# Second batch's kept-pair transpositions ordered after the first batch's last probabilities on VectorE

## The chip, the cores and the metric

The kernel runs on one core of one Trainium2 chip. The metric is the device time of one execution in microseconds (us). Three runs of the kernel before gave 949.78, 950.34 and 950.64 us; the median is 950.34 us. TensorE (PE in the profile) multiplies matrices into accumulators in PSUM; VectorE (DVE), ScalarE (ACT) and GpSimd (POOL) work on elements; SyncE (SP) issues transfers (DMA) between memory and the core's SBUF. Every engine executes its own instructions in the order in which the program lists them, and waits where an operand is not there yet.

## The reference

Eight batches of attention (8 heads, 576 positions, width 64) are followed by a gated feed-forward layer over all 4608 tokens. Heads 0 to 3 see the last 32 positions, heads 4 to 7 see every 32nd position back from their own.

```python
scores = scale * np.matmul(q, k.transpose(0, 1, 3, 2))
mask_local = (rel >= 0) & (rel < stride)                      # heads 0..3, stride = 32
mask_strided = (rel >= 0) & (pos[None, :] % stride == pos[:, None] % stride)   # heads 4..7
attn = softmax(np.where(masks, scores, -1e9))
x = np.matmul(attn, v) -> [4608, 512]
h = x @ w_in                                                  # 512 -> 2048
g = h * np.clip(h + 3.0, 0.0, 6.0) / 6.0
out = g @ w_out                                               # 2048 -> 512
```

## The kernel before

**Work units.** Two heads make a pair, four pairs (c = 0 to 3) a batch; pair g is numbered through the batches, so g = 0 to 3 is the first batch and g = 4 to 7 the second. Within the second batch `TURNS` takes the strided pairs first: g = 4 is c = 2 and g = 5 is c = 3. Pairs 0 to 7 go through `kept_pair`, the rest through `pair`. For the feed-forward layer a batch is a tile of 512 tokens (the 64 left over of every batch are collected in `left`), which `ffn` takes in 16 chunks fc of 128 hidden units. Exactness near fp32 is had by splitting every operand into a high and a low part, so that a product is three matmuls: L973, L974, L975 (tile `ph`, the first product) and L931, L932, L933 (tile `acc`, the second).

**A pair's steps in `kept_pair`.** Query and key are loaded (L360, tiles `qn` and `kn`, into one of three buffers `n`) and, for the second batch, transposed on VectorE (`tr`, L492: `qt<-qn` and `kplain<-kn` or `kt<-kn`). For the first batch TensorE transposes them instead. TensorE makes the scores (L551, L554, tile `ps`; two banks of PSUM for the second batch), ScalarE copies the wanted blocks (L568), GpSimd masks them (L587), VectorE takes the maximum (L592), GpSimd subtracts it (L596), ScalarE exponentiates (L599), VectorE sums and inverts (L602 to L607), GpSimd normalises (L611). VectorE then transposes the probabilities in four pieces (`transposes`, L637, tile `atkept<-e`), one set for each head j of the pair, and TensorE multiplies them with the values (L689, tile `pv`). In `keep_x` the result is split: ScalarE writes the high part of `x` (L396), VectorE the low part (L399), first for one half of the tokens and then for the other, in a chain.

**The first tile of `ffn`.** The four first products fc = 0 to 3 are begun before all four pairs are there: each collects the pairs c in the order 0, 2, 1, 3 as they come. fc = 0 and 1 use the two `ph` banks, fc = 2 and 3 the banks of the accumulators 2 and 3:

```python
pk = ("acc", fc) if t == seq[0] and fc in (2, 3) else ("ph", fc % 2)
```

Each then goes through `gated` (ScalarE L985 `u<-ph`, VectorE L989 `u<-u,ph`, called the gate below) and `parts_of` (ScalarE L997 `gh`, GpSimd L1002 `gl`). Only when the gate of fc = 2 has read its bank can the second product write accumulator 2; the second product of one fc is four groups of three matmuls, for accumulators 0 to 3.

**Weights.** A chunk of weights comes as fp32 (L287, `rawi` and `rawo`), is cut apart by ScalarE (L295, L299), joined by VectorE (L303, called a join below), rounded on ScalarE or GpSimd (L309, L311), and GpSimd makes the low part (L315).

**The order is written by a planner.** `Plan.op` records each operation with its engine, its cost, the names of what it reads and writes, a due time, an earliest planned time (`early`) and a further distance to what it depends on (`room`). `Plan.emit` runs a list schedule over these costs: of the engines it takes the one that can start soonest, and there the operation that can start soonest, at equal starts the one with the earlier due time. From one operation to the next there are 0.12 us (0.02 us on the same engine) in this planner's clock, to which `room` is added. The operations are then emitted in the order of their planned starts, and that is the order of each engine's instructions on the chip; the planned times themselves do not reach the chip. The names are free: a name that stands for no tile orders operations in the plan and makes no semaphore.

For the transpositions of query and key `room` is `LATE` = 2.0 and `early` is the later of `due - AHEAD` and `T0 + OPEN`, for g = 4 the planned 50.0. Transfers are planned with 2.2 us (`FETCH`) and a further time of their own between issue and landing.

Of the kernel before, what the change touches and what calls it, by code (L numbers as in the profile page):

```python
# [32 lines left out]
AHEAD = 27.0  # L33
PTPE = 0
BYACT = 8
OPEN = 6.0
# [4 lines left out]
T0 = 44.0  # L41
TILE = 98.5
ROOM = 1.2
LATE = 2.0
# [7 lines left out]
class Plan:  # L52
# [12 lines left out]
    def op(self, engine, us, fn, reads=(), writes=(), due=0.0, room=0.0, mode="", after=0.0, take=None, give=None, early=0.0):  # L65
        n = len(self.ops)
        before = set()
        for k in reads:
            if k in self.wrote:
                before.add(self.wrote[k])  # L70
            self.used.setdefault(k, []).append(n)
        for k in writes:
            if k in self.wrote:
                before.add(self.wrote[k])
            before.update(self.used.pop(k, ()))
            self.wrote[k] = n
        before.discard(n)
        how = engine if isinstance(engine, dict) else {engine: us}
        self.ops.append((how, fn, before, due, room, mode, after, take, give, early))
        return n  # L80
# [85 lines left out]
def attention_ffn(ctx: ExitStack, tc, q, k, v, w_in, w_out, out):  # L166
# [6 lines left out]
    NPAIR = H // 2  # L173
# [14 lines left out]
    op = plan.op  # L188
# [82 lines left out]
    def wkey(w, g, i):  # L271
        return ("w", w, g, i)
# [58 lines left out]
    def psum(key, name):  # L331
        return new(pp, key.key if isinstance(key, Slot) else key, [P, TOK], F32, name)
# [13 lines left out]
    def timing(g):  # L346
        b = g // NPAIR
        if not b:
            return T0 - 6.0 * (NPAIR - g)
        return wanted[b] - 6.0 - (NPAIR - 1 - g % NPAIR) * (wanted[b] - opens[b]) / NPAIR  # L350
# [57 lines left out]
    def kept_pair(g):  # L408
# [3 lines left out]
        loc = h0 < H // 2  # L412
        nm = f"{b}_{c}"
        early = (b == 0) + (g == 0)
        due = timing(g)
# [8 lines left out]
        tkey = {"q": qkey, "k": kkey}  # L424
# [17 lines left out]
        for x in "qk":  # L442
            if early:
                nkey = wkey("io"[x == "k"], NQ - 2, c)
            else:
                nkey = ("n", nn[0] % 3)
                nn[0] += 1

            if early:

                def load(x=x, nkey=nkey):
                    t = new(wp, nkey, [P, NQB, 2, D], F32, f"{x}n{nm}")
                    for j in range(2):
                        (nc.scalar if g == 1 else nc.sync).dma_start(
                            t[:QB, :, j], {"q": q, "k": k}[x][b, h0 + j].rearrange("(i p) d -> p i d", p=QB))
                tb = [slot(early) for _ in range(2)]

                def tr(x=x, nkey=nkey, tb=tb):
                    ps = [psum(tb[h], f"{x}p{nm}{h}") for h in range(2)]
                    for i in range(NQB):  # L460
                        nc.tensor.transpose(ps[i // 3][:, i % 3 * QB:i % 3 * QB + QB],
                                            tiles[nkey][:QB, i].rearrange("p j d -> p (j d)"), tiles["ident",][:QB, :QB])

                def evac(e, x=x, tb=tb, h=0):
                    ps, to, half = tiles[tb[h].key][:, :S // 2], qk_of(x), NPOS // 2
                    if loc:
                        c0 = (PAD if x == "k" else 0) + S // 2 * h
                        to = to[:, c0:c0 + S // 2]
                    else:
                        to = to.rearrange("c (r m) -> c m r", r=STRIDE)[:, half * h:half * h + half]  # L470
                        ps = ps.rearrange("c (m r) -> c m r", r=STRIDE)
                    if e == "ACT":
                        nc.scalar.copy(to, ps)
                    else:
                        nc.vector.tensor_copy(to, ps)
                op("ACT" if g == 1 else "SP", 1.06, load, writes=[nkey], due=-60 + 2 * g + (x == "k") - 900 * (g == 1), after=0.9)
                op("PE", 0.13 * NQB * slow, tr, reads=[("ident",), nkey, "plain", tkey[x]], writes=tb, take=tb, due=due - 1020, mode="s")
                for h in range(2):
                    op({"ACT": 0.45, "DVE": 0.4} if loc else {"ACT": 0.65, "DVE": 0.65}, 0, partial(evac, h=h), reads=[tb[h]],
                       writes=[tkey[x]] if h == 0 else [tkey[x] + (1,) if isinstance(tkey[x], tuple) else tkey[x] + "1"], give=tb[h], due=due - 19)  # L480
                continue

            def load(x=x, nkey=nkey):
                load_qk(x, b, h0, nkey, ap, f"{x}n{nm}")

            def tr(x=x, nkey=nkey):
                to = qk_of(x)
                if loc:
                    to = to[:, PAD if x == "k" else 0:].rearrange("c (m r) -> c m r", r=STRIDE)
                else:  # L490
                    to = to.rearrange("c (r m) -> c m r", r=STRIDE)[:, :NPOS]
                nc.vector.transpose(to, tiles[nkey])  # L492
            op("SP", 2.12, load, writes=[nkey], due=due - 35, early=due - 45, after=2.0)
            op("DVE", 0.8 if loc else 1.25, tr, reads=[nkey, "plain"], writes=[tkey[x]], due=due - 18, early=max(due - AHEAD, T0 + OPEN), room=LATE)


        vkey = wkey("i", NQ - 1, c) if early else ("vt",) if loc else wkey("i", NQ - 1, odd)
# [17 lines left out]
        ekeys = [("el" if loc else "es", j) for j in range(2)]  # L515
        akeys = [("atl", j) for j in range(2)] if loc else [wkey("o", NQ - 1, 0)] * 2
# [18 lines left out]
        for j in range(2):  # L535
# [6 lines left out]
            for i0 in range(0, nblk, 4):  # L542
# [14 lines left out]
                def keep(e, j=j, bkey=bkey, blocks=blocks, i0=i0):  # L557
# [16 lines left out]
                first = i0 == 0  # L574
# [6 lines left out]
                   writes=[ek, st] if first else [ek + (i0,)], give=bkey, due=sd + 0.5)  # L581
# [44 lines left out]
        def transposes(j):  # L626
            def tr():
                at, e = tiles[akeys[j]], e_whole(j)
                if loc:
                    for a in range(3):  # L630
                        for h in range(2):
                            nc.vector.transpose(at[PAD * (a + h):PAD * (a + h) + PAD, :, PAD * a:PAD * a + PAD],
                                                e[PAD * a:PAD * a + PAD, :, PAD * h:PAD * h + PAD])
                else:
                    for a in range(4):
                        rows = slice(PAD * a, PAD * a + PAD)
                        nc.vector.transpose(at[rows, :, rows], e[rows])  # L637

            def whole(half, key):
                ps = psum(key, f"pp{nm}{j}{half}").rearrange("p (u x) -> p u x", x=P)  # L640
                for u in range(nblk // 2):
                    i = half * nblk // 2 + u
                    if loc:
                        nc.tensor.transpose(ps[:2 * PAD, u, :QB], e_whole(j)[:, i], tiles["ident",][:QB, :QB])
                    else:
                        nc.tensor.transpose(ps[:PAD, u], e_whole(j)[:, i], tiles["ident",])

            def parts(half, key):
                ps = tiles[key.key].rearrange("p (u x) -> p u x", x=P)[:, :nblk // 2]
                at = tiles[akeys[j]][:, half * nblk // 2:(half + 1) * nblk // 2]  # L650
                if loc:
                    for a in range(3):
                        for h in range(2):
                            nc.scalar.copy(at[PAD * (a + h):PAD * (a + h) + PAD, :, PAD * a:PAD * a + PAD],
                                           ps[PAD * h:PAD * h + PAD, :, PAD * a:PAD * a + PAD])
                else:
                    for a in range(4):
                        nc.scalar.copy(at[PAD * a:PAD * a + NPOS, :, PAD * a:PAD * a + NPOS],
                                       ps[:NPOS, :, PAD * a:PAD * a + NPOS])
            if j == 0 and g < PTPE:  # L660
                for half in range(2):
                    tb = slot(early)
                    op("PE", 0.08 * slow * nblk / 2, partial(whole, half, tb), reads=[("ident",), ekeys[j]], writes=[tb, akeys[j]], take=tb,
                       due=due - 1002, room=0.0 if early else ROOM, mode="s")
                    op("ACT", 6 * 0.3 if loc else 4 * 0.25, partial(parts, half, tb), reads=[tb], writes=[akeys[j]], give=tb, due=due - 2 + j)
            else:
                op("DVE", 6 * 0.37 if loc else 4 * 0.435, tr, reads=[ekeys[j]], writes=[akeys[j]], due=due - 2 + j)

        if loc:
            transposes(0)  # L670
# [2 lines left out]
            def both():  # L673
                window_products(psum(vb[0], f"pv{nm}0"), psum(vb[1], f"pv{nm}1"), tiles[vkey], [tiles[x] for x in akeys])
            op("PE", 1.3 * slow, both, reads=[*akeys, vkey], writes=[*vb, *xk, lk], take=vb, due=due - 1001,
               room=0.0 if early else ROOM, mode="v")
            keep_x(nm, b, c, [(vb[0], lambda ps: ps, lambda x: x, TOK, False),
                              (vb[1], lambda ps: ps[:, :LEFT], lambda x: x, LEFT, True)], due)
        else:
            for j in range(2):  # L680
                transposes(j)

                def mm(j=j):
# [8 lines left out]
                   due=due - 1001 + j, room=0.0 if early else ROOM, mode="v")  # L692
# [420 lines left out]
```

## Time and profile before

| what | value |
|---|---|
| device time, three runs | 949.78, 950.34, 950.64 us |
| the profiled execution: span from first to last instruction | 949.4 us |
| TensorE busy | 930.3 us (98%) |
| VectorE, ScalarE, GpSimd busy | 593.4, 521.6, 446.0 us |
| the first 80 us: TensorE busy, granted clock | 66.78 us, 0.85 |

Of the profiled execution the span is recorded; its time is that span and what lies around it, which the runs put at 0.4 to 1.2 us (949.78 or 950.64 less 949.4). In the timelines that follow, a row is a start, a duration, an engine, the line of the kernel, the operation, the tile written and the tiles read, and how many instructions are merged; square brackets hold the idle time of that engine just before and what ended it. A row of windows gives a stretch, its length, the busy time of the engine with the number of instructions, the granted TensorE clock as a share of full speed, the share of the DMA engines in use, and GB/s.

### The profile page before, as it was taken

How to read it: one execution, taken by the hardware profiler on the slowest of the kernel's cores; microseconds unless marked ns; L12 is line 12 of the kernel's file. 1: busy time of each engine (PE TensorE's matmuls, PEld its weight loads, DVE VectorE, ACT ScalarE, POOL GpSimd, SP SyncE). 2: the span in 40 equal slices, each digit the busy share in tenths (PEclk: the TensorE clock that was granted, in tenths of full speed). 3: DMA queues.
4: the chain of work that ended last, by engine and by line, in shares of the span. 5: the costliest groups of instructions: out<-in, count | busy, mean ns of one | idle time of the engine just before them, and what ended most of it. 6: DMA issues, size and time to landing. Idle time of an engine off the chain costs nothing.

```text
span 949.4 us, 15283 instructions
## 1 busy us (share of the span) xinstructions
PE 930.3 (98%) x5084; PEld 772.1 (81%) x5084; DVE 593.4 (63%) x1644; ACT 521.6 (55%) x1325; POOL 446.0 (47%) x441
## 2 busy tenths in 40 slices
PE   8869999999999999999999999999999999999997
PEld 8657787888888788988888888888888888888896
DVE  6966677778868776556577687677786873111111
ACT  5747857766665556455346665666556553322332
POOL 5646888554535344434345454544453552222221
PEclk9968999999999999999999999999999999999999
DMA  9658630322222123112112322232223200100000
GB/s 209 211 152 234 159 86 1 86 39 42 52 74 49 32 39 80 22 34 56 27 19 48 72 42 40 42 84 42 40 42 84 42 14 1 45 1 1 33 13 22
DMA packets 197190, 57.16 MB, mean 60 GB/s; under 512 B 188408, under 2 KB 188408, under 8 KB 197112
## 3 DMA queue, kind: packets, MB, share of 16 engines
q1 hardware_dynamic: 194744, 55.61, 25.9%
q10 hardware_dynamic: 2368, 0.59, 0.4%
q8 instruction: 40, 0.66, 0.3%
q14 instruction: 38, 0.31, 0.1%
HBM read 46.73 MB, written 9.44 MB: 59 GB/s over the span
## 4 chain that ended last, share of the span: by engine, by line
PE 91%; SPq 3%; DMA 3%; issue 1%; ACT 1%; DVE 0%; POOL 0%; POOLq 0%; ACTq 0%; DVEq 0%
PE acc L931 13%; PE ph L973 12%; PE acc L932 12%; PE acc L933 12%; PE ph L974 12%; PE ph L975 12%; PE ps L808 3%; PE pv L379 2%; DMA rawi<-in_moe_w_in_dram 2%; PE phl L973 2%; PE phl L975 2%; PE phl L974 2%; PE accl L933 1%; PE accl L931 1%; PE accl L932 1%; PE pv L883 1%
## 5 line engine op out<-in xcount | busy, mean ns | idle before, releaser
L1002 POOL TENSOR_TENSOR gl<-u,gh 128x512 fp32r<-128x512 f32 x128 | 168.8, 1319 | 298.6 <-ACT gh L997 265.1
L973 PE MATMUL ph<-x,wi 128*128 128x512 f32 x512 | 204.3, 399 | 0.0
L931 PE MATMUL acc<-wo,gh 128*128 128x512 f32 x512 | 201.6, 394 | 0.0
L974 PE MATMUL ph<-x,wi 128*128 128x512 f32 x512 | 201.2, 393 | 0.2 <-DVE x L399 0.2
L975 PE MATMUL ph<-x,wi 128*128 128x512 f32 x512 | 201.0, 393 | 0.0
L932 PE MATMUL acc<-wo,gh 128*128 128x512 f32 x512 | 200.0, 391 | 0.0
L933 PE MATMUL acc<-wo,gl 128*128 128x512 f32 x512 | 200.0, 391 | 0.0
L985 ACT ACTIVATE u<-ph,three 128x512 f32<-128x512 f32 x128 | 88.3, 690 | 168.4 <-PE ph L975 167.4
L989 DVE SCALAR_TENSOR_TENSOR u<-u,ph 128x512 f32<-128x512 f32 x128 | 87.7, 686 | 131.4 <-ACT u L985 130.2
L832 ACT ACTIVATE e<-e,st 126x126 f32<-126x126 f32 (+2 forms) x264 | 102.9, 391 | 47.7 <-DVE st L826 45.9
L975 PEld LDWEIGHTS ph<-x,wi 128*128 128x128 f32 x512 | 96.8, 189 | 20.9
L933 PEld LDWEIGHTS acc<-wo,gl 128*128 128x128 f32 x512 | 96.2, 188 | 20.7
L973 PEld LDWEIGHTS ph<-x,wi 128*128 128x128 f32 x512 | 96.7, 189 | 19.6
L931 PEld LDWEIGHTS acc<-wo,gh 128*128 128x128 f32 x512 | 96.3, 188 | 19.4
L932 PEld LDWEIGHTS acc<-wo,gh 128*128 128x128 f32 x512 | 96.3, 188 | 17.9
L974 PEld LDWEIGHTS ph<-x,wi 128*128 128x128 f32 x512 | 96.9, 189 | 17.2 <-DVE x L399 0.7
L997 ACT CAST gh<-u 128x512 fp32r<-128x512 f32 x128 | 79.4, 620 | 55.4 <-DVE u L989 49.9
L848 POOL TENSOR_TENSOR e<-e,st 96x96 f32<-96x96 f32 (+1 forms) x72 | 69.2, 977 | 27.8 <-DVE st L843 26.2
L826 DVE CUSTOM_DVE_ANT_0 e<-ps,e 126x126 f32<-126x126 f32 (+2 forms) x264 | 64.8, 279 | 2.2
L865 DVE STREAM_TRANSPOSE atstr<-e 32x160 f32<-32x160 f32 x168 | 56.3, 335 | 10.0 <-POOL e L848 7.0
L865 DVE STREAM_TRANSPOSE atloc<-e 32x192 f32<-32x192 f32 (+1 forms) x144 | 52.2, 363 | 15.0 <-POOL e L848 12.5
L753 POOL TENSOR_TENSOR qq<-qt,qq 64x576 fp32r<-64x576 f32 x29 | 41.9, 1443 | 36.8 <-ACT qq L749 22.2
(135 smaller groups left out, 1445.8 us busy)
## 6 DMA issues: line engine op xcount, KB each, us to landing
rawi<-in_moe_w_in_dram SPq DMA_DIRECT2D x16, 512.0 KB
rawo<-in_moe_w_out_dram SPq DMA_DIRECT2D x16, 512.0 KB
out_dram<-ob SPq DMA_DIRECT2D x32, 256.0 KB
qn<-in_q_dram SPq DMA_DIRECT2D x112, 72.0 KB
kn<-in_k_dram SPq DMA_DIRECT2D x112, 72.0 KB
vt<-in_v_dram SPq DMA_DIRECT2D x24, 160.0 KB
vt<-in_v_dram SPq DMA_DIRECT2D x120, 31.5 KB
v<-in_v_dram SPq DMA_DIRECT2D x32, 36.0 KB
```

Source lines behind the costliest of these rows:

```text
L832: nc.scalar.activation(e, e, AF.Exp, bias=st_of(j, 0)[:, i:i + 1], scale=-1.0, accum_out=st_of(j, 1)[:, i:i + 1])
L865: nc.vector.transpose(at[ks, i0:, qs], e[qs, i0:, ks])
L931: nc.tensor.matmul(acc, gh, woh, start=fc == 0, stop=False)
L932: nc.tensor.matmul(acc, gh, wol, start=False, stop=False)
L933: nc.tensor.matmul(acc, gl, woh, start=False, stop=end)
L973: nc.tensor.matmul(ph, wih, xh, start=n_ == 0, stop=False)
L974: nc.tensor.matmul(ph, wih, xl, start=False, stop=False)
L975: nc.tensor.matmul(ph, wil, xh, start=False, stop=n_ == NCC - 1)
L985: nc.scalar.activation(u, tiles[pk][:, :n], AF.Relu, bias=three)
L989: nc.vector.scalar_tensor_tensor(out=u, in0=u, scalar=6.0, in1=tiles[pk][:, :n], op0=ALU.min, op1=ALU.mult)
L997: nc.scalar.copy(g, tiles[uk][:, :n])
L1002: eng.tensor_tensor(out=g, in0=tiles[uk][:, :n], in1=tiles[gk[0]][:, :n].bitcast(F32), op=ALU.subtract)
```

## The change

A name `"first"` is written in the plan by the last transposition of probabilities of the first batch (pair 3, head 1), and read by every VectorE transposition of a query or key in `kept_pair`, that is for pairs 4 to 7.

```diff
-            op("DVE", 0.8 if loc else 1.25, tr, reads=[nkey, "plain"], writes=[tkey[x]], due=due - 18, early=max(due - AHEAD, T0 + OPEN), room=LATE)
+            op("DVE", 0.8 if loc else 1.25, tr, reads=[nkey, "plain", "first"], writes=[tkey[x]], due=due - 18, early=max(due - AHEAD, T0 + OPEN), room=LATE)
...
-                op("DVE", 6 * 0.37 if loc else 4 * 0.435, tr, reads=[ekeys[j]], writes=[akeys[j]], due=due - 2 + j)
+                op("DVE", 6 * 0.37 if loc else 4 * 0.435, tr, reads=[ekeys[j]], writes=[akeys[j], "first"] if g == NPAIR - 1 and j else [akeys[j]], due=due - 2 + j)
```

No instruction is added or removed, no tile changes place, and no semaphore is added. In the plan, a query or key of pair 4 can start 2.02 us after the end of the named transposition (0.02 us and `LATE`) at the earliest, and the planner works out the order of everything behind it anew, on all engines.

## The prediction

> **What bounds the kernel now.** I read the stretches of the span first, then what ended TensorE's and VectorE's waits, then the granted clock.
>
> ```profile
> span 949.4 us, 15283 instructions
> ```
>
> ```profile
> 0.00:80.00 80.00, 66.78 (x453) 0.85 0.80 194
> 80.00:250.00 170.00, 170.00 (x940) 1.00 0.35 83
> ```
>
> These are TensorE's windows (columns: stretch, length, busy, granted clock, DMA share, GB/s). From 80 us on TensorE is busy without a break at full clock; before it, 13 us are idle and the clock averages 0.85. So what the change does shows as the time at which TensorE gets through the work of the first 80 us, and is kept to the end if no new wait appears. Next, VectorE's timeline around the change, and the GpSimd and ScalarE rows beside it.
>
> ```profile
> 52.73 0.21 DVE L399 TENSOR_TENSOR left<-pv,left 128x64 fp32r<-128x64 f32 x1
> 56.91 1.15 DVE L492 STREAM_TRANSPOSE qt<-qn 128x576 f32<-128x576 f32 x1 [3.96 <-DMA qn<-in_q_dram]
> 57.92 1.74 DVE L637 STREAM_TRANSPOSE atkept<-e 32x256 f32<-32x256 f32 x4
> 59.69 1.25 DVE L492 STREAM_TRANSPOSE kplain<-kn 128x576 f32<-128x576 f32 x1
> 60.78 0.68 DVE L303 SCALAR_TENSOR_TENSOR fo<-fo,rawo 128x512 int32<-128x512 int32 x1
> 61.67 0.62 DVE L399 TENSOR_TENSOR x<-pv,x 128x256 fp32r<-128x256 f32 x1 [0.21 <-ACT left L396]
> ...
> 66.44 1.19 DVE L492 STREAM_TRANSPOSE qt<-qn 128x576 f32<-128x576 f32 x1 [0.58 <-DMA qn<-in_q_dram]
> 69.80 0.69 DVE L989 SCALAR_TENSOR_TENSOR u<-u,ph 128x512 f32<-128x512 f32 x1 [2.17 <-ACT u L985]
> 76.36 1.26 DVE L492 STREAM_TRANSPOSE kt<-kn 128x576 f32<-128x576 f32 x1 [5.87 <-DMA kn<-in_k_dram]
> 77.46 1.27 DVE L989 SCALAR_TENSOR_TENSOR u<-u,ph 128x512 f32<-128x512 f32 x2
> ```
>
> ```profile
> 52.85 0.43 POOL L611 TENSOR_TENSOR e<-e,st 128x144 f32<-128x144 f32 x1
> ```
>
> ```profile
> 60.97 0.61 ACT L396 CAST x<-pv 128x256 fp32r<-128x256 f32 x1 [7.87 <-PE pv L689]
> ...
> 61.43 0.70 ACT L295 ACTIVATE fi<-rawi 128x512 f32<-128x512 f32 x1
> 62.17 0.67 ACT L299 ACTIVATE rawi<-rawi 128x512 int32<-128x512 uint16 x1
> 62.74 0.59 ACT L396 CAST x<-pv 128x256 fp32r<-128x256 f32 x1
> ```
>
> VectorE is free at 52.94 but its next instruction is pair 4's query, which lands at 56.9. The first batch's last probabilities, normalised at 53.28, wait behind it until 57.92. The rows at 76.36 and 77.46 are a second wait of that kind: pair 5's key lands at 76.3, and behind it stand the gates of chunks 1 and 2, which end at 78.73. TensorE's rows:
>
> ```profile
> 36.35 1.21 PE L689 MATMUL pv<-atkept,v 128*64 128x72 f32 x16
> ...
> 55.29 0.39 PE L975 MATMUL ph<-x,wi 128*128 128x512 f32 x1
> 59.71 2.18 PE L689 MATMUL pv<-atkept,v 128*64 128x72 f32 x16 [4.04 <-DVE atkept L637]
> 62.56 1.95 PE L554 MATMUL ps<-kplain,qt 64*128 64x72 f32 x8 [0.67 <-DVE left L399]
> 65.49 1.98 PE L554 MATMUL ps<-kplain,qt 64*128 64x72 f32 x8 [0.97 <-ACT e L568]
> ...
> 77.09 0.63 PE L973 MATMUL ph<-x,wi 128*128 128x512 f32 x1
> 78.37 0.63 PE L931 MATMUL acc<-wo,gh 128*128 128x512 f32 x1
> ...
> 80.18 0.39 PE L931 MATMUL acc<-wo,gh 128*128 128x512 f32 x1
> ...
> 81.54 0.39 PE L931 MATMUL acc<-wo,gh 128*128 128x512 f32 x1
> ...
> 82.22 0.39 PE L931 MATMUL acc<-wo,gh 128*128 128x512 f32 x1
> ...
> 97.28 1.11 PE L554 MATMUL ps<-kt,qt 64*128 64x72 f32 x8
> ```
>
> ```profile
> 46.40:49.05 2.65, 0.02 (x3) 0.90 1.03 408
> 48.54:51.95 3.41, 2.91 (x33) 0.50 1.02 416
> ...
> 55.67:58.78 3.11, 0.00 (x1) 1.00 0.60 93
> 58.78:79.26 20.48, 17.91 (x66) 0.50 0.49 119
> 65.60:69.03 3.43, 3.43 (x12) 0.50 0.24 50
> ...
> 79.26:82.67 3.41, 3.41 (x16) 1.00 1.04 390
> ```
>
> The late probabilities cost TensorE 4.04 us of idleness, and 3.1 us into it the clock falls to half, until 79.26. A group of three matmuls takes 1.28 us at half clock (77.09 to 78.37) and 0.68 at full (81.54 to 82.22); eight score matmuls take 1.95 and 1.11. Half clock came after both idle stretches (2.65 and 4.04 us), and full clock came back at steps of 3.41 us: at 51.95 after a stretch with 2.91 us of products, but not at 69.03, where TensorE had been busy for all 3.43 us, half of them with scores.
>
> [...]
>
> **The change, part by part.** Nothing is added or removed; the order is. I worked the planner's list on by hand from the code's costs. That clock serves for order only. With T the planned end of the last probability transposition, VectorE's order becomes: one join, the four transpositions, two joins, query 4 (T+2.02), first half of x, key 4, second half of x (ends T+6.06), two joins, gate of chunk 0, query 5, then key 5 and the gates of chunks 1 and 2. Key 5 is planned at 65.07 in both versions: its load stands behind pair 5's values, planned 52.25 to 58.75, and 58.75 + 2.2 + 2.0 + 0.12 + 2.0 = 65.07. T comes out at 54.16, chunk 1's gate at 65.4 and chunk 2's at 66.1. So **key 5 stays ahead of both gates**, by 0.3 and 1.0 of planned time.
>
> Step 1, *the wait removed*. After one join of 0.68 from 52.94, the probabilities take 1.74 and end at about 55.4. TensorE's own products run to 55.5, then the 1.21 us product with the values, to 56.8 instead of 61.89: 5.1 us earlier, 4.04 of them idleness and 1.0 the half clock.
>
> Step 2, *what is late next*. The two halves of x form a chain. The first half's high part ends on ScalarE at 57.5 (0.61); its low part waits for query 4, still landing at 56.9 and done at 58.06, and ends at 58.7. Key 4 (1.25) goes next to 59.9. On ScalarE the second high part now follows three weight steps (two like L295, one like L299, 2.1 us from 57.5) and 0.59 of its own, to 60.2; its low part (0.62) ends at 60.8. TensorE restarts at 60.9, after another 4.1 us of idleness, longer than the 2.65 that halved the clock before. It restarts 1.7 us before 62.56, but the clock falls as it did.
>
> Step 3, *pair 5's key*. SyncE's rows:
>
> ```profile
> 53.02 3.01 SPq L360 DMA_DIRECT2D kn<-in_k_dram  x4
> 56.14 6.44 SPq L511 DMA_DIRECT2D v<-in_v_dram  x8
> 62.62 2.09 SPq L360 DMA_DIRECT2D qn<-in_q_dram  x4
> 64.82 6.85 SPq L511 DMA_DIRECT2D v<-in_v_dram  x8
> 71.78 2.03 SPq L360 DMA_DIRECT2D kn<-in_k_dram  x4
> ```
>
> SyncE issues without a break from 53.02 to 73.81. Key 5 reuses query 4's buffer, which is read by 58.06 in both versions, long before 71.78; its planned place does not move. So it lands at 76.3 as before, and the gates of chunks 1 and 2 end at 78.7 as before. Queued behind them on ScalarE are `gh` of chunk 1 and copies of pair 4's scores.
>
> Step 4, *who waits*. The third group of the second product writes the bank that chunk 2's gate reads. The order on TensorE becomes: product of chunk 0, two score blocks, chunks 1, 2, 3, first part of chunk 4, the third score block, two accumulator groups, then the third group, the fourth score block, the fourth group. At half clock what stands ahead of the third group is 7 x 1.28 + 3 x 1.95 = 14.8 us, from 60.9 to 75.7; if the clock comes back at 69.03 the 6.7 us left shrink by 0.68/1.28, to end near 72.6. Either way TensorE then stands for 3 to 6 us until 78.73. Before, it reached that group at 80.18 without standing. The work done by 78.73 is nearly equal: two groups more (1.36 us at full clock), one score block less (1.11), and before was 0.36 us at half clock into its first group (0.18), which leaves the change 0.07 ahead.
>
> Step 5, *the clock at the restart*. Before, half clock ends 0.53 us after 78.73, a loss of 0.27. After an idleness of 3 to 6 us it starts at half. On the grid of 3.41 us it can return at 82.67 or at 86.08: losses of (82.67 - 78.73)/2 = 1.97 or 3.68. The first window holds a score block of 1.95, like the one at 65.60 that did not bring it back, so I take the second. If it doesn't fall at all, the loss is 0.
>
> **Sum** against the profiled execution: 3.68 - 0.27 - 0.07 = **+3.3**; the bounds are -0.3 (no half clock) and +1.6 (return at 82.67). Chunk 1's gate is within 0.3 of planned time of passing key 5; then chunk 2's comes 0.63 earlier (1.27/2), and all bounds fall by 0.6. I take +2.7. The span would go from 949.4 to 952.1; the runs lie 0.4 to 1.2 above the span, the median 0.9, so **953.0 us**.
>
> [...]
>
> **The rivals.** *A, the gates pass pair 5's key* (ends faster). If the planner gets the gates of chunks 1 to 3 ahead of key 5 (the point is the 1.0 by which I have chunk 2 behind 65.07), TensorE doesn't stand at the third group. It reaches it at 72.6 to 75.7 without the last score block (1.11), against 80.18: 6.5 to 3.4 us saved, so 943.8 to 947. For: chunk 0's product starts earlier than before. Against: by hand, key 5 is ahead, as at 76.36. *B, the 4 us come back as an equal wait and nothing else*: the same landing sets the same gates, and the clock holds, or returns at the first step (82.67, as it did at 51.95 after 2.91 us of work: +1.0 to +1.6, so 951.3 to 951.9, chance 0.10), or other products are listed ahead of the third group. In all -1.0 to +1.6, so 949.3 to 951.9. [...] *C, a further wait.* The third score block's copies stand on ScalarE behind `gh` of chunk 1, so pair 4's softmax starts 5 us later than before; if its product then waits, +5 to +8, so 955 to 958. Against: the products between cover some 3 us of it. *D, nothing moves*: the name is no semaphore, but query 4 can't be planned ahead of T; under 1 in 100, left out.
>
> **How the numbers follow.** My case (half clock to 86.08) 0.45, own range 952.0 to 954.3 (+1.7 to +4.0: the sum with a us of error); A 0.22; B 0.27, of which 0.10 is the return at 82.67; C 0.06. A run of this kernel can be told from no change at about 0.2%, 1.9 us: same is 948.4 to 952.2. Faster: A and 0.02 of B, 0.24; same: the 0.25 left of B and 0.06 of my case, 0.31; slower: 0.39 of my case and C, 0.45. The range takes my case with some half a us above it, B, and the slower half of A: 945.3 to 954.8, leaving out half of A and C, 0.17.
>
> **What would show it.** Right: four probability transpositions at about 53.6 ahead of query 4 at 56.9; the last pair's product near 55.6; TensorE's restart near 61 with chunk 0's product; `kt<-kn` still at 76.4 with two gates behind it; an idle of 3 to 6 us ahead of a group `acc` near 78.8, released by VectorE; granted clock 0.5 for 4 to 7 us after. Wrong: gates ahead of `kt<-kn`, which gives A; no idle before 78.8 or a full clock there, which gives B; a wait of `pv` for `atkept` near 90, which gives C. A key that lands elsewhere than 76.3 would upset step 3 and all that follows.

## The result, and the profile after

| | median of device time | runs |
|---|---|---|
| before | 950.06 us | 948.90 to 950.64, 4 runs |
| after | 956.91 us | 956.81 to 957.32, 4 runs |

The ratio is 1.0080, with a 95% interval of 1.0067 to 1.0093: the change costs 6.9 us, and the forecast of 953.0 us (945.3 to 954.8) had the sign and less than half of the size; the measured time lies 2.1 us above its range. The profiled execution took 956.98 us.

The page of the profile after, with busy times and instructions by engine:

```profile
span 955.2 us, 15271 instructions
...
PE 934.3 (98%) x5084; PEld 772.7 (81%) x5084; DVE 592.3 (62%) x1653; ACT 513.6 (54%) x1316; POOL 443.7 (46%) x441
```

TensorE's work is the same, and no engine is busier in a way that matters; the question is again where TensorE stands, or runs at half clock. One thing did change beside the order: where the kernel leaves the choice of an engine open, the planner chooses with the order, and it chose anew. Of the 48 copies of `ksplit` (high parts of later pairs' keys) VectorE makes 20 instead of 13, and ScalarE the others. VectorE's group after (copies, busy us, mean ns, idle us ahead of them):

```profile
L760 DVE CAST ksplit<-ksplit 64x576 fp32r<-64x576 f32 x20 | 20.2, 1011 | 1.2 <-ACT ksplit L749 0.7
```

VectorE's timeline around the change:

```profile
54.37 1.78 DVE L637 STREAM_TRANSPOSE atkept<-e 32x256 f32<-32x256 f32 x4
...
57.91 1.19 DVE L492 STREAM_TRANSPOSE qt<-qn 128x576 f32<-128x576 f32 x1
...
73.96 1.26 DVE L492 STREAM_TRANSPOSE kt<-kn 128x576 f32<-128x576 f32 x1 [8.10 <-DMA kn<-in_k_dram]
75.06 1.86 DVE L989 SCALAR_TENSOR_TENSOR u<-u,ph 128x512 f32<-128x512 f32 x3
```

The change did what its name says: the four transpositions of probabilities (`atkept`) now stand ahead of pair 4's query (57.91). But VectorE then waits 8.10 us, not 5.87, for pair 5's key, and the gates behind it (`u<-u,ph`, now three) start only at 75.06. TensorE's timeline:

```profile
56.49 1.21 PE L689 MATMUL pv<-atkept,v 128*64 128x72 f32 x16
60.26 0.50 PE L973 MATMUL ph<-x,wi 128*128 128x512 f32 x1 [2.55 <-ACT left L396]
61.24 0.77 PE L974 MATMUL ph<-x,wi 128*128 128x512 f32 x1 [0.48 <-DVE left L399]
...
62.37 2.91 PE L554 MATMUL ps<-kplain,qt 64*128 64x72 f32 x16
...
76.38 0.80 PE L931 MATMUL acc<-wo,gh 128*128 128x512 f32 x1 [4.18 <-DVE u L989]
77.96 1.98 PE L554 MATMUL ps<-kplain,qt 64*128 64x72 f32 x8
```

The wait of 4.04 us ahead of `pv<-atkept,v` is gone, one of 2.55 and 0.48 us comes behind it, and a wait of 4.18 us stands ahead of the third accumulator group, released by the gate of chunk 2: the place that the forecast named. TensorE's windows (stretch, length, busy, granted clock, DMA share, GB/s):

```profile
61.31:68.14 6.83, 6.83 (x25) 0.50 0.39 71
72.20:76.38 4.18, 0.00 (x0) 0.83 0.94 249
74.96:85.20 10.24, 8.82 (x24) 0.50 0.95 270
...
170.00:250.00 80.00, 77.85 (x413) 1.00 0.28 57
```

After the wait 8.82 us of work run at a granted clock of 0.50 (74.96 to 85.20); half of that, by estimate, is the cost: 4.41 us. The last line is the one that was not expected: between 170 and 250 us TensorE is idle for 2.15 us, where before it was busy for all 170 us from 80 to 250. The waits of TensorE from 70 to 260 us (in total, how many, the longest):

```profile
PE acc L931 <- DVE u L989: 4.2, 1, 4.2
PE ps L808 <- POOL ksplit L753: 0.7, 1, 0.7
PE ps L808 <- DVE x L399: 0.5, 1, 0.5
PE acc L932 <- POOL wo L315: 0.4, 1, 0.4
PE ph L973 <- DVE u L989: 0.4, 1, 0.4
PE ps L808 <- DVE ksplit L760: 0.2, 1, 0.2
```

Below the first line stand five small waits, for GpSimd's and VectorE's work on later pairs, weights and gates: operations that the change doesn't name, 100 us and more behind it. They are 2.15 us of idleness together, but cost more. At full clock products that follow each other start 0.23 us apart here, and a row lasts 0.39 us (129.78 to 130.92 of the changed kernel), so by estimate a start that comes late shows as idleness only past the first 0.16 us of its delay. With 0.16 for each, the five waits delay TensorE by 2.95 us.

**Two executions laid over each other.** Their starts differ. SyncE's rows, in the execution after:

```profile
42.66 7.59 SPq L360 DMA_DIRECT2D qn<-in_q_dram  x4
...
54.40 6.44 SPq L511 DMA_DIRECT2D v<-in_v_dram  x8
...
70.04 2.03 SPq L360 DMA_DIRECT2D kn<-in_k_dram  x4
```

and before, the same load of pair 4's query:

```profile
44.92 8.06 SPq L360 DMA_DIRECT2D qn<-in_q_dram  x4
```

SyncE is 2.26 us ahead at 42.66, before anything that the change moves, and pair 5's key comes 2.40 us earlier (73.96 instead of 76.36). Its distance to pair 4's values is what it was: 70.04 - 54.40 = 15.64, and 71.78 - 56.14 = 15.64. So I count from the transposition of that key. "Group n" below is the n-th group of three matmuls of the second product, by the end of its last one; the middle columns are distances from the start of `kt<-kn`.

| | before | after | after less before |
|---|---|---|---|
| group 4 | +6.03 | +7.56 | +1.53 |
| group 16 | +17.59 | +20.94 | +3.35 |
| group 32 | +51.18 | +55.99 | +4.81 |
| group 128 | +200.33 | +209.33 | +9.00 |
| end of the span | +873.07 | +881.23 | +8.16 |

At group 16 the changed kernel also owes one group of the first product (0.68 us) that before had done by then, so the early loss is 4.0 us. By group 32 it is level again, so 0.8 us more come from 16 to 32. At group 128 it is one group of the first product ahead (0.68 of the 9.0 us), so another 3.5 come from 32 to 128, and after that nothing: at the end the loss is 8.2 us, 3.4 more than at group 32. Of these 3.4 the five waits are 2.95. The 8.2 us stand against 6.9 by the medians, or 7.9 against the 17 further runs of before below; a profile is one execution of each kernel, and the rest isn't resolved.

### The profile page after: what moved, and what is told of

It reads as the page before. It is cut to its first block, busy times and chain, and to the rows that moved or that the text cites. A ratio compares the mean times of both kernels' runs of the same rounds, so it can differ in the third digit from the quotient of the medians.

```text
span 955.2 us, 15271 instructions
## 1 busy us (share of the span) xinstructions
PE 934.3 (98%) x5084; PEld 772.7 (81%) x5084; DVE 592.3 (62%) x1653; ACT 513.6 (54%) x1316; POOL 443.7 (46%) x441
## 4 chain that ended last, share of the span: by engine, by line
PE 88%; SPq 3%; DMA 3%; DVE 2%; issue 2%; ACT 1%; POOL 1%; ACTq 0%; POOLq 0%; DVEq 0%
PE acc L931 12%; PE acc L932 12%; PE acc L933 12%; PE ph L973 12%; PE ph L974 11%; PE ph L975 11%; PE ps L808 3%; PE pv L379 2%; PE phl L973 2%; PE phl L975 1%; PE phl L974 1%; PE accl L933 1%; PE accl L931 1%; PE accl L932 1%; PE pv L883 1%
## 5 line engine op out<-in xcount | busy, mean ns | idle before, releaser
L832 ACT ACTIVATE e<-e,st 96x128 f32<-96x128 f32 (+2 forms) x264 | 102.8, 391 | 33.8 <-DVE st L826 33.4
L826 DVE CUSTOM_DVE_ANT_0 e<-ps,e 96x128 f32<-96x128 f32 (+2 forms) x264 | 64.3, 278 | 2.3
```

The source lines that it names most:

```text
L832: nc.scalar.activation(e, e, AF.Exp, bias=st_of(j, 0)[:, i:i + 1], scale=-1.0, accum_out=st_of(j, 1)[:, i:i + 1])
```

## The experiments

Theory **T1**: two separate losses. One is early: pair 5's key ahead of the gates, with the wait and half clock behind it. The other is late, and comes with the new order of everything behind: the planner, given one new dependence, wrote another list for the rest of the kernel, and in that list some operations stand where TensorE waits for them. Rival **T2**: all of it comes from the early stretch, and the later waits only show that the kernel arrives there late. In the quoted texts "Theory 1", "Theory 2" and "Rival" are the answers to the question that the run in hand asks.

To try parts alone, the planner is run twice, with and without the change's dependence (`hold`). What the one plan starts before a planned time `CUT` is emitted in its order, and what is left in the other plan's order. An operation's engine goes with the plan that it is taken from. The planned times are not the chip's: the cut at the planned 130 us falls at 141 to 147 us of TensorE's rows, the cut at 90 at 98 to 104.

```diff
+        early, late = self.schedule(EARLY), self.schedule(REST)
+        head = [x for x in early[0] if x[0] < CUT]
+        done = {x[2] for x in head}
+        rest = [x for x in late[0] if x[2] is not None and x[2] not in done]
```

All times are compared with runs of the kernel before on the same chip: 949.03 us (17 runs) for the first four kernels, 949.15 (28) for the second four and 949.62 (29) for the last four.

| kernel | median us | ratio to before (95%) |
|---|---|---|
| h_early | 955.10 | 1.0059 (1.0042 to 1.0075) |
| h_late | 953.63 | 1.0051 (1.0036 to 1.0066) |
| k_key5 | 951.85 | 1.0030 (1.0021 to 1.0040) |
| e_warm | 955.24 | 1.0075 (1.0057 to 1.0093) |
| h_key5 | 949.71 | 1.0007 (0.9995 to 1.0020) |
| h_key5_only | 951.28 | 1.0026 (1.0012 to 1.0040) |
| h_early_fill | 953.15 | 1.0047 (1.0033 to 1.0061) |
| h_key5_fill | 949.81 | 1.0006 (0.9990 to 1.0023) |
| he_90 | 953.26 | 1.0033 (1.0022 to 1.0044) |
| hk_90 | 948.35 | 0.9989 (0.9979 to 0.9999) |
| h_late5 | 955.03 | 1.0059 (1.0043 to 1.0075) |
| h_nudge | 951.91 | 1.0024 (1.0013 to 1.0035) |

### The early half and the late half

h_early takes the change's order up to the planned 130 us and before's order from there on:

```diff
+EARLY, REST, CUT = True, False, 130.0
```

> The planner is run twice, without and with the new name; what the second plan starts before its 130 us is emitted in the second plan's order, all the rest in the first plan's. So the early order is that of the change and the late order that of the kernel before. Theory 1 (the loss has two parts: about 2.4 us at 72 to 85 us from the wait for the gate behind pair 5's key and the half clock after it, and about 3.3 us between 170 and 235 us from a late order that the planner made anew): 952.5 us, with the wait of some 4 us ahead of a group acc near 76 still there and no further loss after 100 us. Theory 2 (the second part follows from being late, whatever the order): about 956.9 us, with waits again between 170 and 235 us.

h_late is the reverse: before's order up to 130, the change's from there on.

```diff
+EARLY, REST, CUT = False, True, 130.0
```

> The reverse: the early order is that of the kernel before, the order of what is planned from 130 us on that of the change. Theory 1: 950.1 plus the 3.3 us of the late order, about 953.4 us, with TensorE as before up to 110 us and waits at score products between 170 and 235 us. Theory 2: about 950.1 us.

Waits and a window of TensorE in h_early:

```profile
PE acc L952 <- DVE u L1010: 4.5, 1, 4.5
```

```profile
170.00:250.00 80.00, 80.00 (x428) 1.00 0.28 57
```

Waits of TensorE in h_late, 70 to 260 us:

```profile
PE ps L829 <- POOL ksplit L774: 0.7, 1, 0.7
PE ph L994 <- DVE u L1010: 0.7, 2, 0.4
PE ps L829 <- DVE x L420: 0.5, 1, 0.5
PE acc L953 <- POOL wo L336: 0.4, 1, 0.4
```

(Lines are some 20 further down in these kernels.) h_early has the early wait and none of the late ones, though it arrives 5.3 us late at group 48 in its profile. h_late is not late at all at group 16 (0.2 us, counted from the key), and has four of the five late waits of the changed kernel at the same instructions, and one more of its own. So the late waits go with the late list, not with lateness, and T2 falls on that point. The list is order and choice of engines together (h_late has VectorE make 20 copies of `ksplit`, h_early 13); which of the two makes the waits was not tried. Each half alone costs more than its share in the whole: 6.1 and 4.6 us by the medians. They don't add up to the 6.9 to 7.9 that the change costs (956.91 less 950.06 or 949.03). T1's times were 953.4 for h_late, near the measured 953.63, and 952.5 for h_early, 2.6 us too low. Both were counted from 950.1 us, and the runs of before on that chip have 949.03: as losses, T1's 2.4 and 3.3 us are 6.1 and 4.6. So T1 has the places right and both sizes too small.

### Pair 5's key held behind the gates

k_key5 is the change, with the key of pair 5 planned no earlier than 69.0, behind the gates of chunks 1 and 2 (of the line, the argument that changes):

```diff
-early=max(due - AHEAD, T0 + OPEN)
+early=69.0 if g == 5 and x == "k" else max(due - AHEAD, T0 + OPEN)
```

> The change, with pair 5's key held back in the plan to 69 us, so that the gates of chunks 1 to 3 stand ahead of it on VectorE. Theory 1 (the gates wait only for that key's landing): the 4.2 us wait of TensorE near 72 is gone, the clock does not fall a second time, and TensorE is 5 to 9 us further on at 100 us than with the change; the late order is planned anew, worth 0 to 3 us either way: 946 to 951 us. Rival (the gates or the bank would have been late anyway, by ScalarE or the accumulators): 955 to 957 us with a wait at the same place.

TensorE's windows in it:

```profile
62.01:68.84 6.83, 6.83 (x24) 0.50 0.40 73
68.84:78.00 9.16, 9.16 (x46) 1.00 0.66 165
...
170.00:250.00 80.00, 77.41 (x437) 1.00 0.27 55
```

and its two longest waits from 70 to 260 us:

```profile
PE ps L808 <- DVE x L399: 1.4, 1, 1.4
PE ph L973 <- DVE u L989: 1.4, 2, 0.8
```

The wait of 4.2 us and the second stretch at half clock are gone (granted clock 1.00 from 68.84 to 78.00): the key was their cause. Counted from the key, this kernel leads before by 5.0 us at group 16. Then the lead melts, to 2.0 us at group 64, and at group 96 it is 1.7 us behind, with waits that its own new list brings. It comes out 0.9 us above its first range.

h_key5 keeps that early order and takes before's order from the planned 130 on; h_key5_only holds the key but leaves the change's dependence out:

```diff
+EARLY, KEY5, REST, CUT = True, True, False, 130.0
```

> The early order (planned starts before 130 us) of the run with pair 5's key held back to 69 us behind the new name, and the late order of the kernel before. Theory 1 (what that run gave back between 130 and 235 us was its newly made late order): its lead of some 5 us at 90 us is kept, 943 to 945 us against 949.0 of before. Theory 2 (a TensorE that is 5 us early there runs into loads and engines that come at their own time): 947.5 to 951 us, with waits between 100 and 235 us.

```diff
+EARLY, KEY5, REST, CUT = False, True, False, 130.0
```

> The kernel before with only pair 5's key held back to 69 us in the early plan, without the new name, and the late order of before. If that key costs only where TensorE reaches the third accumulator before the gates are through (it does with the change, not before): within 1 us of the kernel before, 948 to 950 us. Rival (the key held up the kernel before as well): 945 to 947.5 us.

Waits of TensorE in h_key5 behind 70 us:

```profile
PE acc L966 <- POOL gl L1037: 2.0, 2, 1.7
PE ps L839 <- DVE st L857: 0.7, 1, 0.7
PE ps L582 <- DVE left L430: 0.5, 1, 0.5
```

h_early lies 6.1 us above its runs of before and h_key5 0.6, with one planned time changed: 5.5 us is the price of the key's place in this order. Yet it is not faster than before, as Theory 2 had it. Its lead, counted from the key, is 5.05 us at group 16; 2.43 are left at group 48 and 1.43 at group 80. The gates come so early that the next to be late is their low part, which GpSimd makes (`gl`, 1.7 us), and the rest goes in two small waits and in changes of TensorE between scores and products: twelve between groups 32 and 48, where before has eight. Without the change's dependence the key's place gains nothing: by the medians h_key5_only is 2.1 us slower than before, against both of its numbers. In the trace of before the gates' wait of 5.87 us for the key is covered by products (TensorE has no wait from 70 to 260 us); in the change it isn't (4.18 us). But executions of one order differ: the profiled execution of h_key5_only is the fastest of its ten (948.10 us, the median 951.28), its mean granted clock is 0.990 where before's is 0.987, TensorE reached the third group at 73.59, ahead of the key at 75.28, and it leads before by 5.0 us at group 16 and by 2.0 at the end. Where the median's 2.1 us are lost no trace shows; that stays open.

### The clock

e_warm is the change with 30 products of the identity, into a free bank, ahead of the third group, where TensorE stands for 4.2 us:

```diff
+                        if fc == 0 and i == 2 and t == seq[0]:
+                            fill(("s", 1), 30)
```

> The change, with 30 matmuls of the identity with itself ahead of the third group of the second product, into a score bank that is free there, to fill most of the 4.2 us for which TensorE waits. Same order otherwise. If the half clock from 75 to 85 us costs what it seems to (8.8 us of work at half clock after the restart, 4.4 us): 952.5 us, with full clock after the wait. If the activity of such matmuls doesn't keep the clock, or something else paces that stretch: 956 to 957 us.

Its windows, in and behind the added products:

```profile
72.38:79.24 6.86, 6.86 (x62) 1.00 0.82 227
79.24:85.20 5.96, 5.96 (x30) 1.00 1.16 274
```

The granted clock stays at 1.00. The added products last 6.86 us and end about 1.3 us behind the gate of chunk 2; counted from the key, the execution is 2.8 us ahead of the changed kernel at group 16. With the 1.3 that is 4.1 us for the clock, near the estimate of 4.41 for the half clock. By the medians the gain is smaller, 1.7 us (956.91 to 955.24), or 0.6 where each is taken against its own runs of before (6.85 and 6.21). The lead of 2.8 us lasts to the end (2.9 there), and 1.4 of it is missing in the two profiled times because the key of this execution lands at 75.33 instead of 73.96. So the trace bears out the estimate for the clock; the medians lie between the two numbers of the text, nearer to the second, and whether the later start is chance isn't settled.

h_early_fill puts 17 such products into h_early, h_key5_fill 10 into h_key5, ahead of its first group that follows the idle stretch at 57 us:

```diff
+FILL1, FILL2 = 0, 17
```

> Early order of the change, late order of before, and 17 matmuls of the identity in the 4.2 us wait ahead of the third group (each is two passes of 0.117 us, 4.0 us in all; the 30 of the run before ran 1.3 us past the gate). The half clock after the restart, 8.8 us of it, goes: 4 us less than without the filling, 955.1 - 4.1 = 951 us. If the clock isn't the cause: 955 us.

```diff
+FILL1, FILL2 = 10, 0
```

> As the early order with pair 5's key held back and the late order of before, with 10 matmuls of the identity (2.3 us) in the 2.5 us that TensorE stands before the product of chunk 0. If they keep the clock, the half clock of 6.8 us that starts there goes, worth 3.4 us: 3 us below that run. If the gates, the weights or the landing of a key pace that stretch instead: less than 1 us below it.

h_early_fill's windows:

```profile
79.18:86.01 6.83, 6.83 (x21) 0.50 1.12 271
75.46:77.96 2.50, 0.00 (x0) 1.00 0.93 300
```

17 products left 2.5 us idle, and the clock fell behind it all the same, for 6.83 us of work instead of the 8.43 of h_early (76.86 to 87.10): the kernel lies 2 us below h_early, in the middle between the two numbers. The shorter half clock is worth, by estimate, (8.43 - 6.83)/2 = 0.8 us of that, and counted from the key the trace ends 0.6 us ahead of h_early's; the rest of the 2 us is in no trace. h_key5_fill gains nothing (949.81 against 949.71): TensorE then waits 2.5 us for `gl` instead of 1.7, and the mean granted clock of the profiled execution is 0.990, no higher than the 0.992 of h_key5.

### Where the late loss begins, and whether any new list costs

he_90 and hk_90 are h_early and h_key5 with the cut at the planned 90 us instead of 130:

```diff
+EARLY, KEY5, REST, CUT = True, False, False, 90.0
```

> The early order of the change up to the planned 90 us, then the order of the kernel before, SyncE's whole order included. It has two changes of TensorE between scores or values and the feed-forward products more than before, where the mixture at 130 us has six more. Theory 1 (early loss 4.1 us from the wait and the half clock, 0.4 us for each such change): 4.1 + 0.8 = 4.9 us above before, 1 to 2 us below the mixture at 130 us (955.1): 953 to 954.2 us. Theory 2 (the early loss is all of it and such changes cost nothing): as the mixture at 130 us, 955 us.

```diff
+EARLY, KEY5, REST, CUT = True, True, False, 90.0
```

> The same cut at 90 us with pair 5's key held back too, so that the gates pass it; as many changes of TensorE's kind as before. The profile of the mixture at 130 us had a lead of 5 us at 95 us and gave back 3.6 by 200 us, 1.5 of it waits and some 1.6 four further changes. Theory 1: those changes are gone, and 2 to 4 us of lead stay: 945 to 947.5 us, the fastest of all. Theory 2 (what comes at its own time takes the lead back): 948.5 to 950 us with new waits before 200 us.

Against their own runs of before, he_90 (+3.6 us) lies 2.4 us below h_early (+6.1), and hk_90 (-1.3) 1.8 below h_key5 (+0.6): the stretch from the planned 90 to 130 us in the changed list costs something of its own. In the traces he_90 ends 1.4 us ahead of h_early, 0.8 of it between groups 32 and 48, where h_early has ten changes between scores or values and products and he_90 eight. he_90 comes out in Theory 1's range (953 to 954.2), hk_90 a little under Theory 2's. hk_90 holds the key back for a gain of 4.9 us over he_90, close to the 5.5 above. It is the only version that beats before, by 0.1% (ratio 0.9989, up to 0.9999), hardly more than a measurement can tell. Its profiled execution is not typical, the slowest of its twelve (951.49 us): by estimate it lost 3.4 us, half of the 6.82 us of work at a granted clock of 0.50 from 101.15 to 107.97 (last section). Its first wait is again GpSimd's:

```profile
PE acc L966 <- POOL gl L1037: 2.3, 1, 2.3
```

h_late5 keeps before's order up to 130 and takes the rest from the plan with the change and the held key; h_nudge does so with a plan in which only pair 8's query is planned 2 us later:

```diff
+EARLY, KEY5, REST, CUT = False, False, True, 130.0
```

> The early order of the kernel before, and from the planned 130 us on the order that the planner makes when only pair 5's key is held back, with the new name. Theory 1 (any late order made anew is worse than that of the kernel before, whose TensorE stands 0.6 us in 870): 951.5 to 954.5 us with waits between 140 and 240 us. Rival (the late order of the change is worse for a reason of its own): 948.5 to 950 us.

```diff
+        if nudge:
+            avail[self.nudge] += 2.0
```

> The early order of the kernel before, and from the planned 130 us on the order that the planner makes without the new name when one transposition alone, the query of pair 8, can start 2 us later in the plan. Nothing in it has to do with the change. Theory 1: as above, 951 to 954.5 us. Rival: 948.5 to 950 us.

A window of TensorE in h_late5:

```profile
170.00:250.00 80.00, 77.06 (x434) 1.00 0.28 57
```

With before's own early stretch, each of the three new lists for the rest costs: h_late 4.6 us, h_late5 5.4, h_nudge 2.3. That is above Theory 1's range for h_late5 (951.5 to 954.5) and in it for h_nudge (951 to 954.5). The nudge has nothing to do with the change. So the late loss is not a property of this dependence: before's list has nearly no waits (170.00 of 170.00 us busy from 80 to 250), and each other list that was tried has some. They don't lose at one place: h_nudge is only 0.4 us behind before at group 128, counted from the key, and 2.9 at group 192. Three lists are a small sample; that every other list costs isn't shown.

## Why the forecast was right in sign and wrong in size

- **Step 1, right.** The transpositions ran from 54.37 to 56.15 (forecast: to 55.4), and the last product with values began at 56.49 (forecast: 55.5), without a wait.
- **Step 2, right in kind.** Forecast was a restart at 60.9 after 4.1 us of idleness; it was 60.26 after 2.55, with 0.48 more before the second matmul. The clock fell to 0.50 at 61.31, as forecast.
- **Step 3, right.** Key 5 stayed ahead of the gates of chunks 1 and 2 (and of a third one). It landed at 73.96 instead of 76.3, but SyncE was 2.26 us ahead before anything that the change moves, so that is this execution and not the change.
- **Step 4, right.** TensorE's order was as worked out, to the last group, and the wait ahead of the third was 4.18 us, in the 3 to 6.
- **Step 5, right in mechanism, mis-sized.** The clock was to be half until the later of the two steps of the grid that I named; it was (85.20). The loss was, by estimate, 4.41 us instead of 3.68. By the same formula, 4.41 - 0.27 - 0.07 = 4.07, which is the 4.0 measured at group 16. Forecast was +2.7, since I took 0.6 off for a gate that might pass the key. None passed it. The other 0.7 is where the restart (76.38) fell in the stretch at half clock (74.96 to 85.20), and that was luck.
- **"Kept to the end if no new wait appears", wrong.** That is the sentence that failed. I had worked the planner's order on only to about 90 us, and rival C looked for a further wait at pair 4's product with its values. The sum has nothing for what is behind that. It came at 175 to 235 us in places that the change doesn't name, 3.4 us behind group 32. h_early and h_late show that it is the list there, and not the early loss carried on. The measured 956.91 lies in rival C's 955 to 958, but by luck: C's wait did not come, since TensorE was busy for all 90.00 us from 80 to 170.
- **Missing: 0.8 us between groups 16 and 32.** TensorE is never idle there. The segment takes 35.04 us instead of 33.59, with one group of three matmuls more (0.68) and with two more changes between scores and products of the feed-forward part. What such a change cost stands in the trace of before:

```profile
96.97 0.39 PE L975 MATMUL ph<-x,wi 128*128 128x512 f32 x1
97.28 1.11 PE L554 MATMUL ps<-kt,qt 64*128 64x72 f32 x8
...
98.66 0.39 PE L974 MATMUL ph<-x,wi 128*128 128x512 f32 x1
...
100.27 0.39 PE L933 MATMUL acc<-wo,gl 128*128 128x512 f32 x1
100.59 1.62 PE L554 MATMUL ps<-kt,qt 64*128 64x72 f32 x16
...
102.47 0.39 PE L932 MATMUL acc<-wo,gh 128*128 128x512 f32 x1
```

  From the matmul ahead to the second one behind, eight scores take 98.66 - 96.97 = 1.69 us and sixteen 102.47 - 100.27 = 2.20. Two plain steps of 0.23 are in both, so eight scores add 0.51 and going there and back 1.69 - 0.46 - 0.51 = 0.72. One such excursion more and the 0.68 give 1.40 of the 1.45 us.
- **The offset to the device time.** I put 0.9 us around the span, from runs that were not the profiled one; this execution has 956.98 - 955.2 = 1.8, and the profiled ones of the experiments have 1.8 to 1.9. The 949.4 us of before belongs then, by estimate, to an execution of about 951.2, and not to the median.
- **Rival A, wrong in what it would give.** With the gates ahead of the key the early gain is real (k_key5: 5.0 us at group 16, counted from the key; A had 3.4 to 6.5), but the time came out at 951.85 and not at 943.8 to 947.

What stays open: h_early and h_late alone cost 1.7 us (traces) to 3.8 us (medians) more together than the change; 0.9 of the 1.7 lies between groups 32 and 48, where the two lists meet. Some 0.4 us of the late 3.4 lie in no wait that the trace shows. More changes between kinds of matmul are not behind it: from group 32 on before has 314 between scores or values and products, the change 310. And one of the eight executions of h_early took 949.86 us, one of the twelve of he_90 949.01, which is 5.2 and 4.3 below their medians; no trace of them was kept, so what they were spared isn't known.

## What to carry to other kernels

Where a planner writes the order, a new dependence is a new list from there to the end, engines included: compare both lists on all engines over the whole kernel, or hold the later part to the old order, before a local gain is believed. An operation that waits for a transfer held up here what stood behind it in its engine's queue (8.10 us for pair 5's key on VectorE, ahead of three gates), so look at what is queued behind it, and move that ahead (5.5 and 4.9 us here, behind the change's order; nothing by the median without it). A gain ahead of a stretch in which TensorE is busy all the time held here only until the next engine was late (GpSimd's `gl`, 1.7 us in h_key5), and an extra change between short scores and long products cost 0.72 us there and back (before, 96.97 to 102.47).

## What the runs showed of the hardware

In the traces before and after, the stretches between two changes of the granted clock were, from 34 to 86 us, 1, 2, 3, 5 and 6 times 3.41 us long: before, 3.41 us at 0.50 (48.54 to 51.95), 6.83 at 1.00 and 20.48 at 0.50 (58.78 to 79.26); after, 10.24 at 0.50 (34.00 to 44.24), 17.07 at 1.00, 6.83 at 0.50 (61.31 to 68.14), 6.82 at 1.00 and 10.24 at 0.50 (74.96 to 85.20). And **busy was not enough**. Windows of TensorE in hk_90, whose profiled execution lost its clock at 101.15:

```profile
97.74:101.15 3.41, 2.95 (x26) 1.00 0.91 110
101.15:104.56 3.41, 3.41 (x14) 0.50 0.76 185
104.56:107.97 3.41, 3.41 (x9) 0.50 0.04 16
```

TensorE stood for only 0.46 us in the first of them, and the clock fell at its end. Behind the second, busy for all 3.41 us, it was still at 0.50; behind the third it was back. In its timeline the scores, 64 rows deep, take 2.4 us of the first window and 2.1 of the second:

```profile
98.28 1.62 PE L585 MATMUL ps<-kt,qt 64*128 64x72 f32 x16
100.36 2.93 PE L582 MATMUL ps<-kplain,qplain 64*96 64x128 f32 x16 [0.46 <-ACT e L599]
```

The third holds 128-row products only. The other returns, window by window, with the time of scores (`ps`) in each: in the changed kernel the clock was still at half behind 61.31 to 64.72 (2.35 us of scores) and back behind 64.72 to 68.14 (0.56 us); after the long wait, still at half behind 78.37 to 81.78 (1.57 us) and back behind 81.78 to 85.20 (none). Before, it was still at half behind each of the three windows from 65.61 to 75.85, busy throughout with 1.90, 1.93 and 1.98 us of scores, and back at 79.26 behind the next, which has none. In he_90 the clock even fell without any idleness, behind a window that was busy for all 3.42 us:

```profile
16.24:19.66 3.42, 3.42 (x33) 1.00 1.21 277
19.66:23.07 3.41, 3.41 (x19) 0.50 1.02 405
```

So in these runs the busy time of a window alone does not tell the clock behind it. What does is not shown.

Two further things. The executions before and after, whose list is the same up to there, differ in when SyncE issues pair 4's query, 44.92 against 42.66 us. So single profiles are laid over each other at a common event, not at zero. And in e_warm 60 passes of 0.11 us over a 128 by 128 identity (6.86 us, 72.38 to 79.24) held the granted clock at 1.00 where the kernel had nothing to do.
